# First-layer weight preparation and value pooling in a fused attention and two-layer feed-forward kernel: later value loads summed by GpSimd, weight slices in three steps

## The chip, the cores and the metric

The kernel runs on one core of a Trainium2 chip. The metric is the device time of one execution in microseconds (us). A core has TensorE (PE; its weight loads are listed as PEld), VectorE (DVE), ScalarE (ACT), GpSimd (POOL) and SyncE (SP), which issues the DMA transfers. Each engine works through its own instructions in the order in which the program emits them, and waits where an operand is not ready or a buffer is not free.

## The reference

Three stages follow each other. The attention pools keys and values over 8 neighbouring rows first:

```python
k_p = k.reshape(B, H, Sp, pool, D).mean(axis=3)      # B, H, S, D = 8, 8, 576, 64; pool = 8
v_p = v.reshape(B, H, Sp, pool, D).mean(axis=3)
scores = (1 / sqrt(D)) * q @ k_p.T                   # softmax over the 72 pooled keys
x = softmax(scores) @ v_p                            # then to 4608 tokens of width 512
```

Then come two feed-forward layers, 512 to 2048 to 512, with weights of their own:

```python
h = x @ w_in;   x = (h * clip(h + 3, 0, 6) / 6) @ w_out
h = x @ w_in2;  x = (P(h) / Q(h)) @ w_out2           # P cubic, Q = 1 + |b0||h| + |b1| h*h + 1e-6
```

## The kernel before, in words

**Tiling.** The 4608 tokens are handled in 9 blocks of 512. A feed-forward layer goes through the 16 slices m of the hidden width for each block: `hidden` (line 447) computes 128 hidden rows for 512 tokens with 12 matmuls, an activation follows on ACT and VectorE, and `out1` (line 473; `out2`, 553, in layer two) adds the slice to the four output banks with 12 matmuls, two steps later (LAG = 2). Matmuls are done on a high and a low part of each operand (names ending in h and l), three products each.

**The order of the work.** It is written out by hand. The program is a sequence of steps ("slots"), one per slice and block: steps 0 to 143 are layer one, 144 to 287 layer two, and steps -12 to -1 (PRE = 12) are a prologue in which the attention of the first block and the first weights are made ready. `at(kind, step, function, ...)` puts a piece of work on a list of a step, and `slot(s)` emits the lists in a fixed order. For s >= 0 it is: `dm` (loads), `hidden(s)`, `ex` (exponentials), the second half of the activation of s-1, `el` (pooling), `ld` (more loads), `pe` (transposes, scores, attention), `out1(s-2)`, `nz` (normalisation), `mid` (splits into high and low), `hi` (row maxima), the first half of the activation of s, then `c2`, `c1`, `c3` and `la`. For s < 0 it is dm, ld, el, pe, hi, ex, nz, c1, mid, c2, c3, la. What one engine does in a step follows this order, and nothing later passes it.

**Attention.** Query tiles (`load_q`) go through `scores` (line 333, PE), `highest` (348, VectorE), `exponentials` (355 to 361, ACT), `normalize` (369 VectorE, 370 and 376 GpSimd), `transposes` (385, PE), `split_p` (396 ACT, 397 and 401 VectorE), `attend` (414, PE) and `split_x` (425, 426). Values come in six chunks of 128 rows by 512 per batch. The first batch's chunks are loaded in step -12 (`load_v`, line 235, issued before the second weight slice) into halves of weight tiles that are not yet needed (`half`), and `pool_first_v` (273) sums eight rows with eight matmuls against the identity into a PSUM bank, two chunks in each of steps -11, -10 and -9. The profile counts each of these f32 matmuls as two. `split_v` (287, 288), `mask_v` (297, GpSimd) and `mask_rest` (308 to 313) then make `vh`, `vl` and `vr`, which `attend` reads. Later batches load each chunk into `vraw` (two buffers) one step ahead of `pool_v` (248, a VectorE reduction).

**Weights.** They come as 64-bit values and are decoded on the chip. A layer-one slice (32 of them: m = 0 to 15, w_in and w_out in turn, numbered i = 0 to 31) is loaded (`load_weights`, 148), decoded (`decode_a` 154 and `decode_r` 159, ACT), put together (`decode_b` 173 and 174, VectorE; `decode_c` 181, GpSimd) and split into high and low (`split_weights` 201 ACT, 203 GpSimd or VectorE). Slices 0 to 23 take three steps for this: c3 of step s-1, c1 of s, c2 of s+1, slice 23 without the last. Slices 24 to 31 go through `make_ready(i)`, all in c1 of one step: decode slice i, split slice i-1, put slice i together. Their loads are in `ld` of step s-1, and s = 2(i-11)/3 rounded down, so that four slices fall on three steps. Slices 24, 25, 28 and 29 are loaded into the two halves of the tile `y`, slices 26, 27, 30 and 31 into the two `raw64` buffers. All eight share the single buffer `t` (line 172) for the assembled value.

Of the kernel before, what the change touches and what calls it, by code (L numbers as in the profile page):

```python
# [19 lines left out]
F32 = mybir.dt.float32  # L20
F32R = mybir.dt.float32r
I32 = mybir.dt.int32
U32 = mybir.dt.uint32
I64 = mybir.dt.int64
AF = mybir.ActivationFunctionType
ALU = mybir.AluOpType
AX = mybir.AxisListType

B, H, S, D = 8, 8, 576, 64
POOLED = 8  # L30
SP = S // POOLED
NT, DM, DFF = B * S, H * D, 2048
P = 128
# [8 lines left out]
VCH = 6  # L42
# [26 lines left out]
def feed_forward_kernel(tc, q_t, k_t, v_r, vmask, w_in1, w_out1, w_in2, w_out2, a_rep, b_rep, out):  # L69
    nc = tc.nc  # L70

    const = tc.alloc_tile_pool(name="const", bufs=1)
    wpool = tc.alloc_tile_pool(name="weights", bufs=1)
# [4 lines left out]
    att = tc.alloc_tile_pool(name="att", bufs=1, side="right")  # L78
    dram = tc.alloc_tile_pool(name="spill", bufs=1, space=bass.MemoryType.DRAM)
    ps_y = tc.alloc_tile_pool(name="ps_y", bufs=1, space=bass.MemoryType.PSUM)  # L80
# [7 lines left out]
    ident = const.tile([P, P], F32, name="ident")  # L88
    vr = const.tile([P, 2, 2, 2, D], F32R, name="vr")
    kbd = const.tile([P, NPAIR, 2, SP], F32, name="kbd")  # L90
    mask = const.tile([P, 6], F32, name="mask")
# [32 lines left out]
    LATE = MF // 2  # L124
# [4 lines left out]
    def place(m, o):  # L129
        return wpool.tile([P, 2, DM], F32R, tag=f"w{m}{o}", name="w")  # L130

    def early(c):
        return c[0] == 0 and c[1] < AT_WORK
# [16 lines left out]
    def decode_a(*c):  # L150
        hi = raw[c].bitcast(I32).rearrange("p (n t) -> p n t", t=2)[:, :, 1].bitcast(F32)

        dec[c] = ps_h.tile([P, DM], F32, tag="h", name="d") if c[0] == 0 and 2 * c[1] + c[2] < PRE - 1 else hi
        nc.scalar.activation(out=dec[c], in_=hi, func=AF.Copy, scale=2.0 ** -112)

    def decode_r(*c):
        lo = raw[c].bitcast(I32).rearrange("p (n t) -> p n t", t=2)[:, :, 0]
        rnd[c] = lo
        nc.scalar.activation(out=lo, in_=lo.bitcast(U32), func=AF.Copy, scale=2.0 ** -29)
# [3 lines left out]
    def decode_b(*c):  # L163
        d = dec.pop(c).bitcast(I32)
        if early(c):
            i = 2 * c[1] + c[2]
            if i % 2 == 0:
                m, o = RAWS[NRAW + i // 2 % 2]
                turns[0] = wpool.tile([P, 2, DM], I32, tag=f"w{m}{o}", name="t")
            t = turns[0][:, i % 2, :]  # L170
        else:
            t = att.tile([P, DM], I32, tag="t", name="t")
        nc.vector.tensor_scalar(out=t, in0=d, scalar1=3, scalar2=None, op0=ALU.logical_shift_left)
        nc.vector.scalar_tensor_tensor(
            out=t, in0=d, scalar=-2 ** 31, in1=t, op0=ALU.bitwise_and, op1=ALU.bitwise_or
        )
        whole[c] = t

    def decode_c(*c):
        t = whole[c]  # L180
        nc.gpsimd.tensor_tensor(out=t, in0=t, in1=rnd.pop(c), op=ALU.add)  # L181
        whole[c] = t.bitcast(F32)
# [14 lines left out]
    def split_weights(*c):  # L197
        t = whole.pop(c)
        raw.pop(c)
        w = place(*c[1:])  # L200
        nc.scalar.activation(out=w[:, 0, :], in_=t, func=AF.Copy)
        eng = nc.gpsimd if c[2] or 2 * c[1] + c[2] >= PRE - 1 else nc.vector
        eng.tensor_tensor(out=w[:, 1, :], in0=t, in1=w[:, 0, :].bitcast(F32), op=ALU.subtract)
        for i, part in enumerate("hl"):
            wts[part][c] = w[:, i, :]


    q_sb, k_raw, v_raw, vh, vl = {}, {}, {}, {}, {}
# [16 lines left out]
    def half(name):  # L225
        if halves[1] % 2 == 0:
            i = halves[1] // 2
            halves[0] = wpool.tile([P, 2, DM], F32, tag=f"w{LATE + i // 2}{i % 2}", name=name)
        halves[1] += 1
        return halves[0][:, (halves[1] - 1) % 2, :]  # L230

    def load_v(b, c):
        t = half("v_raw") if b == 0 else att.tile([P, DM], F32, tag="vraw", bufs=2, name="v_raw")
        v_raw[b, c] = t.rearrange("p (r d) -> p r d", d=D)
        nc.sync.dma_start(out=t, in_=v_r[b, c])

# [5 lines left out]
    vsum = {}  # L242
# [23 lines left out]
            dst = kbd[rows, :, j, SM:SP] if p == NPAIR else kbd[rows, p, j, 0:SM]  # L266
            nc.vector.tensor_reduce(out=dst, in_=k[rows], axis=AX.X, op=ALU.add)

    def pool_first_v(c):
        if c == 0:  # L270
            vsum[0] = ps_y.tile([P, 512], F32, tag="y0", name="ps_vs")
        for r in range(POOLED):
            nc.tensor.matmul(
                vsum[0][:, c * D:(c + 1) * D], lhsT=ident, rhs=v_raw[0, c][:, r, :],
                start=r == 0, stop=r == POOLED - 1,
            )

    vparts = {}

    def split_v(b):  # L280
        src = vsum.pop(b)
        vs = src
        if b == 0:
            src = src[:, 0:VCH * D].rearrange("p (c d) -> p c d", d=D)
            vs = att.tile([P, VCH, D], F32, tag="vsum", name="vsum")
        vsh = att.tile([P, VCH, D], F32R, tag="vsh", name="vsh")
        nc.scalar.activation(out=vsh, in_=src, func=AF.Copy)
        nc.vector.tensor_tensor(
            out=vs[:, 0:4, :], in0=src[:, 0:4, :], in1=vsh[:, 0:4, :].bitcast(F32), op=ALU.subtract
        )  # L290
        vparts[b] = vsh.bitcast(F32), vs, src

    def mask_v(b, f, part):
        src, dst, nm = vparts[b][part], (vh, vl)[part], ("vh", "vl")[part]
# [9 lines left out]

    def mask_rest(b):

        hi, vs, src = (x[:, 4:6, :] for x in vparts[b])
        nc.vector.tensor_scalar(out=hi, in0=hi, scalar1=mask[:, 3:4], scalar2=None, op0=ALU.mult)
        nc.vector.scalar_tensor_tensor(
            out=vs, in0=src, scalar=mask[:, 2:3], in1=hi, op0=ALU.mult, op1=ALU.add  # L310
        )
        for i in range(2):
            nc.vector.tensor_scalar(
                out=vr[:, :, i, 1, :], in0=vs, scalar1=mask[:, 4 + i:5 + i], scalar2=None, op0=ALU.mult
            )
# [252 lines left out]
    pe, ex, el, nz, mid, hi, la, dm, ld, c1, c2, c3 = ({} for _ in range(12))  # L568

    def at(kind, slot, f, *a):  # L570
        kind.setdefault(slot, []).append(lambda: f(*a))
# [3 lines left out]
    chunks = [(m, o) for m in range(MF) for o in range(2)]  # L575

    def prepare_first(s0, units):

        at(dm, s0, load_q, *units[0])
        for p in (0, 1, NPAIR):  # L580
            at(dm, s0, load_first_k, p)
        at(dm, s0, load_weights, 0, *chunks[0])
        for u in units[1:3]:
            at(dm, s0, load_q, *u)
        for p in (2, 3):
            at(dm, s0, load_first_k, p)
        for c in range(VCH):
            at(dm, s0, load_v, 0, c)
            at(pe, s0 + 1 + c // 2, pool_first_v, c)
        at(dm, s0, load_weights, 0, *chunks[1])  # L590
        for p in (0, NPAIR, 1):
            at(el, s0, pool_first_k, p)
        for p in (2, 3):
            at(la, s0 + p - 2, pool_first_k, p)
        at(la, s0 + 3, split_v, 0)
        for i in range(4):
            at(la, s0 + 4 + i // 2, mask_v, 0, i // 2, i % 2)
        at(la, s0 + 4, mask_rest, 0)

    def prepare(b, k0, k1, a0, a1):  # L600

# [16 lines left out]
    for j in range(NB):  # L618
        s0 = MF * (j - 1)
# [6 lines left out]
        for us in groups:  # L626
            b, g, f, _ = us[0]
            for u in us + [None]:
                s = s0 + round(14 * k / (steps - 1)) if j else k + 2 - PRE
# [26 lines left out]
            prepare(j, k0, k1, a0, a1)  # L656


    def make_ready(i):
        if i < len(chunks):  # L660
            decode_a(0, *chunks[i])
            decode_r(0, *chunks[i])
        here = i < len(chunks) and early((0, *chunks[i]))
        if i > 0 and not here:
            split_weights(0, *chunks[i - 1])
        if i < len(chunks):
            decode_b(0, *chunks[i])
            decode_c(0, *chunks[i])
        if i > 0 and here:
            split_weights(0, *chunks[i - 1])  # L670

    for i in range(len(chunks) + 1):
        s = i + 1 - PRE if i < PRE - 1 else 2 * (i + 1 - PRE) // 3
        c = (0, *chunks[i]) if i < len(chunks) else None
        if c and i > 1:
            if i < 24:
                at(dm, max(s - 3, -PRE), load_weights, *c)
            else:
                at(ld, s - 1, load_weights, *c)
        if i < 24:  # L680

            at(c3, s - 1, decode_a, *c)
            at(c3, s - 1, decode_r, *c)
            at(c1, s, decode_b, *c)
            at(c1, s, decode_c, *c)
            if i < 23:
                at(c2, s + 1, split_weights, *c)
        else:
            at(c1, s, make_ready, i)


    SWITCH = T1 - MF
# [13 lines left out]
    for i, (m, o) in enumerate(chunks):  # L706
        s = 24 + 3 * i
        at(dm, s - 2, load_weights, 1, m, o)
        at(el, s, decode_a, 1, m, o)
        at(la, s + 1, decode_r, 1, m, o)  # L710
        at(la, s + 1, decode_b, 1, m, o)
        at(la, s + 2, decode_c, 1, m, o)
        at(la, s + 3, spill_weights, 1, m, o)
        at(dm, SWITCH + m + 1 + LAG * o, reload_weights, 1, m, o)
    for j in range(NB2):
        s = T1 + j * MF
# [127 lines left out]
```

## Time and profile before

| | us |
|---|---|
| median of 3 runs | 1764.97 |
| lowest and highest | 1764.26, 1765.46 |
| profiled execution | 1760.91 |
| its span, first to last instruction | 1759.2 |

The mean granted TensorE clock over the span is 0.989 of full speed. A row of a timeline reads: start in us, duration in us, engine, line, operation, output <- inputs, partitions x elements, how many; in brackets the idle time of the engine just before and what ended it. A row of the waits reads: who waited <- for whom: total us, how often, longest. A row of the chain of waits reads: start, duration, what. A row of the groups or of a windows view is explained where it stands.

### The profile page before, as it was taken

To read this page: it belongs to the slowest core of one execution; us is meant where nothing else is said; L and a number is where in the kernel's file an instruction comes from. 1 tells how busy PE (TensorE), PEld (TensorE's weight loads), DVE (VectorE), ACT (ScalarE), POOL (GpSimd) and SP (SyncE) were. 2 spreads that over 40 slices of the span, in tenths; PEclk is the share of its full clock that TensorE was granted. 3 is DMA by queue.
4 is the path that set the end of the run, shared out by engine and by line. 5 is a ranking of instruction groups with operands and counts; after the bars stand their busy time and mean duration, and the time that the engine had idled before them with its cause. 6 is when DMAs were issued, how large, how long until landed. Compare 5 with 4: busy or idle time off the path is not lost.

```text
span 1759.2 us, 22444 instructions
## 1 busy us (share of the span) xinstructions
PE 1712.7 (97%) x7824; PEld 1417.2 (81%) x7824; DVE 1065.9 (61%) x1743; ACT 986.5 (56%) x2226; POOL 750.7 (43%) x762
## 2 busy tenths in 40 slices
PE   6688999999999999999999999999999999999999
PEld 5477888888888888888888888888888888888887
DVE  5885546556474664644322666666666666666665
ACT  5776444555455555544322666666666666666665
POOL 4575021212112121211001666666666666767665
PEclk8799999999999999999999999999999999999999
DMA  6532313233241423312055201010101010101000
GB/s 208 176 128 75 94 51 131 77 112 108 86 142 58 140 88 105 118 65 70 13 181 207 91 7 42 7 43 7 42 7 42 7 42 7 44 6 43 1 25 24
DMA packets 68336, 128.33 MB, mean 73 GB/s; under 512 B 11392, under 2 KB 27776, under 8 KB 68224
## 3 DMA queue, kind: packets, MB, share of 16 engines
q1 hardware_dynamic: 68224, 126.91, 21.6%
q8 instruction: 62, 1.02, 0.2%
q14 instruction: 50, 0.41, 0.1%
HBM read 91.23 MB, written 35.65 MB: 72 GB/s over the span
## 4 chain that ended last, share of the span: by engine, by line
PE 90%; DVE 0%; ACT 0%; POOL 0%; issue 0%; DVEq 0%
PE ps_h L447 42%; PE ps_o L553 22%; PE ps_y L473 21%; PE ps_s L333 2%; PE ps_v L414 2%; PE ps_t L385 1%; ACT s L358 0%; POOL gl L539 0%; POOL t L181 0%; DVE t L515 0%; DVE g L530 0%; DVE r L526 0%; DVE qd L523 0%; DVE t L514 0%; ACT y L479 0%
## 5 line engine op out<-in xcount | busy, mean ns | idle before, releaser
L473 PE MATMUL ps_y<-gh,w 128*128 128x512 f32 x1152 | 388.6, 398 | 0.0
L447 PE MATMUL ps_h<-xh,w 128*128 128x512 f32 x1152 | 380.2, 391 | 5.2 <-DVE gl L462 5.2
L447 PE MATMUL ps_h<-x2h,w 128*128 128x512 f32 x1152 | 377.8, 389 | 0.8 <-DVE t L515 0.8
L553 PE MATMUL ps_o<-w,gh 128*128 128x512 f32 x1152 | 354.7, 389 | 0.0
L447 PEld LDWEIGHTS ps_h<-xh,w 128*128 128x128 f32 x1152 | 217.2, 189 | 51.1 <-DVE gl L462 5.8
L473 PEld LDWEIGHTS ps_y<-gh,w 128*128 128x128 f32 x1152 | 217.0, 188 | 46.3 <-issue 1.6
L447 PEld LDWEIGHTS ps_h<-x2h,w 128*128 128x128 f32 x1152 | 216.3, 188 | 46.1 <-DVE t L515 1.2
L553 PEld LDWEIGHTS ps_o<-w,gh 128*128 128x128 f32 x1152 | 216.3, 188 | 45.0
L370 POOL TENSOR_TENSOR s<-s,rc 128x128 f32<-128x128 f32 (+1 forms) x80 | 32.0, 400 | 501.8 <-DVE rc L369 439.4
L523 DVE SCALAR_TENSOR_TENSOR qd<-qd,r 128x512 f32<-128x512 f32 x144 | 99.0, 688 | 220.0 <-ACT r L522 204.4
L473 PE MATMUL ps_y<-gl,w 128*128 128x512 f32 x576 | 225.1, 391 | 0.0
L447 PE MATMUL ps_h<-xl,w 128*128 128x512 f32 x576 | 225.0, 391 | 0.1
L447 PE MATMUL ps_h<-x2l,w 128*128 128x512 f32 x576 | 224.1, 389 | 0.0
L553 PE MATMUL ps_o<-w,gl 128*128 128x512 f32 x576 | 224.1, 389 | 0.0
L510 POOL TENSOR_SCALAR qd<-ah,coef 128x512 f32<-128x512 f32 x144 | 111.3, 773 | 258.2 <-ACT ah L508 258.1
L462 DVE TENSOR_TENSOR gl<-ps_h,gh 128x512 fp32r<-128x512 f32 x144 | 99.4, 690 | 167.3 <-ACT gh L461 166.6
L539 POOL TENSOR_TENSOR gl<-g,gh 128x512 fp32r<-128x512 f32 x144 | 186.6, 1296 | 19.0 <-ACT gh L538 18.9
L513 POOL TENSOR_TENSOR qd<-qd,ah 128x512 f32<-128x512 f32 x144 | 187.1, 1299 | 12.1
L508 ACT ACTIVATE ah<-ps_h 128x512 f32<-128x512 f32 x144 | 86.1, 598 | 152.4 <-PE ps_h L447 152.4
L521 ACT ACTIVATE r<-qd,cst 128x512 f32<-128x512 f32 x144 | 99.6, 692 | 105.2 <-POOL qd L513 105.2
L461 ACT ACTIVATE gh<-ps_h 128x512 fp32r<-128x512 f32 x144 | 84.9, 590 | 113.4 <-PE ps_y L473 97.6
L455 DVE SCALAR_TENSOR_TENSOR ps_h<-r,ps_h 128x512 f32<-128x512 f32 x144 | 100.0, 694 | 75.1 <-ACT r L454 72.5
(87 smaller groups left out, 2646.2 us busy)
## 6 DMA issues: line engine op xcount, KB each, us to landing
raw<-w_in SPq DMA_DIRECT2D x32, 512.0 KB, 3.7
raw<-w_out SPq DMA_DIRECT2D x32, 512.0 KB, 3.7
w<-raw SPq DMA_DIRECT2D x32, 512.0 KB, 2.8
w<-w SPq DMA_DIRECT2D x32, 512.0 KB, 4.1
v_raw<-v_r SPq DMA_DIRECT2D x47, 256.0 KB, 4.0
y<-y SPq DMA_DIRECT2D x36, 256.0 KB, 2.9
x2r<-y SPq DMA_DIRECT2D x36, 256.0 KB, 2.9
out<-o SPq DMA_DIRECT2D x36, 256.0 KB, 2.2
```

The costliest lines, as they stand in the source:

```text
L447: nc.tensor.matmul(ps, lhsT=w, rhs=x, start=o == 0, stop=o == len(ops) - 1)
L455: nc.vector.scalar_tensor_tensor(out=ps, in0=r, scalar=1.0, in1=ps, op0=ALU.min, op1=ALU.mult)
L461: nc.scalar.activation(out=gh[it], in_=ps, func=AF.Copy)
L462: nc.vector.tensor_tensor(out=gl[it], in0=ps, in1=gh[it].bitcast(F32), op=ALU.subtract)
L473: nc.tensor.matmul(yp[j][c], lhsT=w, rhs=x, start=m == 0 and o == 0, stop=m == MF - 1 and o == 2)
L508: nc.scalar.activation(out=ah, in_=ps, func=AF.Abs)
L510: nc.gpsimd.tensor_scalar(out=qd, in0=ah, scalar1=absb[1], scalar2=absb[0], op0=ALU.mult, op1=ALU.add)
L513: nc.gpsimd.tensor_tensor(out=qd, in0=qd, in1=ah, op=ALU.mult)
L521: nc.scalar.activation(out=r0, in_=qd, func=AF.Ln, scale=2.0 ** -LN_SHIFT, bias=cst[:, 1:2])
L523: nc.vector.scalar_tensor_tensor(out=qd, in0=qd, scalar=1.0 + 1e-6, in1=r0, op0=ALU.add, op1=ALU.mult)
L539: nc.gpsimd.tensor_tensor(out=gl[it], in0=g, in1=gh[it].bitcast(F32), op=ALU.subtract)
L553: nc.tensor.matmul(yp[j][c], lhsT=w, rhs=x, start=m == 0 and o == 0, stop=m == MF - 1 and o == 2)
```

## The change

First value batch: `load_first_v(c)` loads two chunks into one whole weight tile (w10,1, then w11,0 and w11,1), and SP issues these loads behind the second weight slice, in steps -12, -11 and -10. `sum_first_v(c)` sums the eight rows of two chunks on GpSimd by three halvings (additions of 512, 256 and 128 elements per partition), at the end (`la`) of steps -11, -10 and -9. The pooling matmuls and their PSUM bank are gone. `split_v`, `mask_v` and `mask_rest` of this batch come one step later and read SBUF.

Late weight slices: `make_ready` is gone. Slices 23 to 31 follow the rule of the others: decode in c3 of step s-1, put together in c1 of s, split in c2 of s+1. The loads of slices 24 to 31 stay in `ld` of step s-1. `t` has two buffers, and `vraw` of the later batches has one instead of two.

```diff
-            t = att.tile([P, DM], I32, tag="t", name="t")
+            t = att.tile([P, DM], I32, tag="t", bufs=2, name="t")
...
+    def load_first_v(c):
+        i = c // 2 + 1
+        v_raw[0, c] = wpool.tile([P, 2, DM], F32, tag=f"w{LATE + 2 + i // 2}{i % 2}", name="v_raw")
+        for i in range(2):
+            nc.sync.dma_start(out=v_raw[0, c][:, i, :], in_=v_r[0, c + i])
...
-        t = half("v_raw") if b == 0 else att.tile([P, DM], F32, tag="vraw", bufs=2, name="v_raw")
+        t = att.tile([P, DM], F32, tag="vraw", name="v_raw")
...
-    def pool_first_v(c):
+    def sum_first_v(c):
         if c == 0:
-            vsum[0] = ps_y.tile([P, 512], F32, tag="y0", name="ps_vs")
-        for r in range(POOLED):
-            nc.tensor.matmul(
-                vsum[0][:, c * D:(c + 1) * D], lhsT=ident, rhs=v_raw[0, c][:, r, :],
-                start=r == 0, stop=r == POOLED - 1,
-            )
+            vsum[0] = att.tile([P, VCH, D], F32, tag="vsum", name="vsum")
+        t = v_raw.pop((0, c)).rearrange("p c (r d) -> p c r d", d=D)
+        n = POOLED // 2
+        while n:
+            dst = t[:, :, 0:n] if n > 1 else vsum[0][:, c:c + 2, :].unsqueeze(2)
+            nc.gpsimd.tensor_tensor(out=dst, in0=t[:, :, 0:n], in1=t[:, :, n:2 * n], op=ALU.add)
+            n //= 2
...
-        for c in range(VCH):
-            at(dm, s0, load_v, 0, c)
-            at(pe, s0 + 1 + c // 2, pool_first_v, c)
         at(dm, s0, load_weights, 0, *chunks[1])
+        for c in range(0, VCH, 2):
+            at(dm, s0 + c // 2, load_first_v, c)
+            at(la, s0 + 1 + c // 2, sum_first_v, c)
...
-        at(la, s0 + 3, split_v, 0)
+        at(la, s0 + 4, split_v, 0)
         for i in range(4):
-            at(la, s0 + 4 + i // 2, mask_v, 0, i // 2, i % 2)
-        at(la, s0 + 4, mask_rest, 0)
+            at(la, s0 + 5 + i // 2, mask_v, 0, i // 2, i % 2)
+        at(la, s0 + 5, mask_rest, 0)
...
-        if i < 24:
+        if True:
             at(c3, s - 1, decode_a, *c)
             at(c3, s - 1, decode_r, *c)
             at(c1, s, decode_b, *c)
             at(c1, s, decode_c, *c)
-            if i < 23:
-                at(c2, s + 1, split_weights, *c)
-        else:
-            at(c1, s, make_ready, i)
+            at(c2, s + 1, split_weights, *c)
```

More of the change, by code (lines that the diff above doesn't have):

```diff
@@ L267, in pool_first_k @@
             nc.vector.tensor_reduce(out=dst, in_=k[rows], axis=AX.X, op=ALU.add)
-    def pool_first_v(c):
+    def sum_first_v(c):
         if c == 0:
-            vsum[0] = ps_y.tile([P, 512], F32, tag="y0", name="ps_vs")
-        for r in range(POOLED):
-            nc.tensor.matmul(
-                vsum[0][:, c * D:(c + 1) * D], lhsT=ident, rhs=v_raw[0, c][:, r, :],
-                start=r == 0, stop=r == POOLED - 1,
-            )
+            vsum[0] = att.tile([P, VCH, D], F32, tag="vsum", name="vsum")
[5 more added lines that the diff above has]
+            n //= 2
     vparts = {}
     def split_v(b):
[L281 to L285, printed above, removed]
+        vs = vsum.pop(b)
         vsh = att.tile([P, VCH, D], F32R, tag="vsh", name="vsh")
-        nc.scalar.activation(out=vsh, in_=src, func=AF.Copy)
+        nc.scalar.activation(out=vsh, in_=vs, func=AF.Copy)
         nc.vector.tensor_tensor(
-            out=vs[:, 0:4, :], in0=src[:, 0:4, :], in1=vsh[:, 0:4, :].bitcast(F32), op=ALU.subtract
+            out=vs[:, 0:4, :], in0=vs[:, 0:4, :], in1=vsh[:, 0:4, :].bitcast(F32), op=ALU.subtract
         )
-        vparts[b] = vsh.bitcast(F32), vs, src
+        vparts[b] = vsh.bitcast(F32), vs
     def mask_v(b, f, part):
@@ L305, in mask_rest @@
     def mask_rest(b):
-        hi, vs, src = (x[:, 4:6, :] for x in vparts[b])
+        hi, vs = (x[:, 4:6, :] for x in vparts[b])
         nc.vector.tensor_scalar(out=hi, in0=hi, scalar1=mask[:, 3:4], scalar2=None, op0=ALU.mult)
         nc.vector.scalar_tensor_tensor(
-            out=vs, in0=src, scalar=mask[:, 2:3], in1=hi, op0=ALU.mult, op1=ALU.add
+            out=vs, in0=vs, scalar=mask[:, 2:3], in1=hi, op0=ALU.mult, op1=ALU.add
         )
@@ L656, in feed_forward_kernel @@
             prepare(j, k0, k1, a0, a1)
[L659 to L672, printed above, removed]
+    for i in range(len(chunks)):
         s = i + 1 - PRE if i < PRE - 1 else 2 * (i + 1 - PRE) // 3
-        c = (0, *chunks[i]) if i < len(chunks) else None
-        if c and i > 1:
+        c = (0, *chunks[i])
+        if i > 1:
             if i < 24:
```

## The prediction

> **What bounds the kernel now.** I read the page first, then the waits of TensorE (PE), once over the whole span and once from 180 us on.
>
> ```profile
> span 1759.2 us, 22444 instructions
> PE 1712.7 (97%) x7824; PEld 1417.2 (81%) x7824; DVE 1065.9 (61%) x1743; ACT 986.5 (56%) x2226; POOL 750.7 (43%) x762
> ```
> ```profile
> PE ps_t L385 <- POOL s L376: 9.3, 2, 6.2
> ...
> PE ps_s L333 <- ACT s L358: 6.4, 4, 2.6
> ```
> ```profile
> PE ps_h L447 <- DVE t L515: 0.8, 1, 0.8
> ```
>
> PE is busy 97% of the span. Its longest waits are for normalised scores in the prologue (first row of the second view); the 6.4 us for ACT are looked at below. The last row is everything PE waits for after 180 us. So every microsecond won or lost ahead of 180 us comes out at the end one for one, and a delay on another engine after that costs nothing until it reaches PE. The change can only pay in two places: the prologue (before the first hidden step, at about 65 us) and steps 0 to 14 of the first layer.
>
> Next I read PE's timeline for the idle time inside the steps, and ScalarE's (ACT's) at the same moments.
>
> ```profile
> 131.94 0.48 PE L414 MATMUL ps_v<-pth,vh 128*128 128x448 f32 x1 [1.15 <-ACT s L358]
> 147.71 0.70 PE L333 MATMUL ps_s<-kbd,q_sb 128*64 128x144 f32 x4 [2.56 <-ACT s L358]
> 163.29 1.33 PE L333 MATMUL ps_s<-kbd,q_sb 128*128 128x144 f32 x4 [2.58 <-ACT s L358]
> ```
> ```profile
> 129.81 0.63 ACT L201 ACTIVATE w<-t 128x512 fp32r<-128x512 f32 x1 [1.86 <-POOL t L181]
> 145.58 0.63 ACT L201 ACTIVATE w<-t 128x512 fp32r<-128x512 f32 x1 [2.90 <-POOL t L181]
> 161.16 0.63 ACT L201 ACTIVATE w<-t 128x512 fp32r<-128x512 f32 x1 [2.91 <-POOL t L181]
> ```
>
> Each of the three PE waits follows an ACT wait by a microsecond or two. `make_ready` puts a slice's split (L201) into the step in which GpSimd (POOL) adds that slice together. ACT stands still until POOL is done, the exponentials (L358) queued behind the split come late, and PE waits for the bank that they read. The chain of waits shows what the last of the three adds:
>
> ```profile
> 164.62 3.79 PE ps_y L473 x12
> ...
> 178.22 2.72 PE ps_y L473 x12
> ...
> 183.99 0.49 PE ps_s L333 x4
> 184.48 2.74 PE ps_y L473 x12
> ```
>
> After the wait of 2.58 us the score matmuls take 1.33 us instead of 0.49 and the twelve output matmuls 3.79 instead of 2.74: PE ran at a lower clock for a while. A step's period is 184.48 - 178.22 = 6.26 us.
>
> **The last eight slices in three steps.** With decode (ACT) in step s-1, bit work and add (VectorE, POOL) in s and split in s+1, no split follows its own add directly. The three waits, 1.15 + 2.56 + 2.58 = 6.29 us, lose their cause, and so do the slow matmuls, 0.84 + 1.05 = 1.89 us: 8.18 us in all. The second t buffer belongs to this. With one, VectorE's bit work waited for the previous slice's split:
>
> ```profile
> 147.58 0.43 DVE L173 TENSOR_SCALAR t<-raw 128x512 int32<-128x512 int32 x1 [3.45 <-POOL w L203]
> ```
>
> With two it waits for the split of the slice before that one, which lies in an earlier step or earlier in the same one.
>
> What is late next: loads keep their step s-1, but the decode moves into that same step. Slices 24 to 27 find fresh buffers, and SP runs ahead. Slice 28 takes over the tile of 24 and 25, whose last reader is 25's add:
>
> ```profile
> 138.51 1.30 POOL L181 TENSOR_TENSOR t<-t,raw 128x512 int32<-128x512 int32 x1 [1.32 <-issue]
> ```
> ```profile
> 139.84 0.33 SPq L148 DMA_DIRECT2D raw<-w_in  x1
> ```
> ```profile
> raw<-w_in SPq DMA_DIRECT2D x32, 512.0 KB, 3.7
> ```
>
> The load leaves at the end of the add and lands 3.7 us later. Carrying the durations of these rows through steps 9 and 10, I put the add's end 2.6 us into step 10, the landing at 6.3 us and ACT's arrival at that decode at 4.6 us: a new ACT wait of about 1.7 us (an estimate). Queued behind it are step 11's exponentials, whose bank PE wants about 3 us into step 11. That is nearly covered, and I charge 0.6 us, for it and for step 11, where ACT has two splits and two decodes. Bounds: nothing, and 2.56 us, the worst wait of the same shape today. Net for this part: 8.2 - 0.6 = **7.6 us won**.
>
> **The first values on POOL instead of PE.**
>
> ```profile
> 13.24 3.65 PE L273 MATMUL ps_vs<-k_raw,ident 128*128 128x64 f32 x16 [1.09 <-DMA k_raw<-v_r]
> ...
> 20.09 0.85 PE L385 MATMUL ps_t<-ident,s 128*128 128x128 f32 x3
> 20.73 1.17 PE L333 MATMUL ps_s<-kbd,q_sb 128*128 128x144 f32 x4
> ...
> 26.00 0.50 PE L385 MATMUL ps_t<-ident,s 128*128 128x128 f32 x3
> 26.34 0.66 PE L333 MATMUL ps_s<-kbd,q_sb 128*128 128x144 f32 x4
> ...
> 39.91 0.79 PE L414 MATMUL ps_v<-ptl,vh 128*128 128x512 f32 x1 [2.07 <-DVE ptl L397]
> ```
> ```profile
> 17.56 0.62 ACT L154 ACTIVATE d<-raw 128x512 f32<-128x512 f32 x1 [4.09 <-DMA raw<-w_out]
> 26.54 0.49 ACT L396 ACTIVATE pth<-ps_t 128x384 fp32r<-128x384 f32 x1 [1.68 <-PE ps_t L385]
> 30.55 0.49 ACT L287 ACTIVATE vsh<-ps_vs 128x384 fp32r<-128x384 f32 x1 [1.88 <-PE ps_vs L273]
> ```
> ```profile
> 6.89 0.43 SPq L235 DMA_DIRECT2D k_raw<-v_r  x1
> ...
> 11.79 0.40 SPq L148 DMA_DIRECT2D raw<-w_out  x1
> ```
>
> Today the pooling matmuls stand ahead of the first transposes (13.24 to 20.09 us). ACT also waits 4.09 us for the second weight slice, which SP issues behind six value loads. In SP's new order that slice leaves where the first value load left, 4.9 us sooner, so its 4.09 us go. The two other ACT waits also end on PE's pooling, directly or through the transposes behind it. This is up to 4.09 + 1.68 + 1.88 = 7.65 us on ACT, but POOL now takes the work over, and POOL decides when the masked values are there:
>
> ```profile
> 15.25 1.29 POOL L181 TENSOR_TENSOR t<-t,raw 128x512 int32<-128x512 int32 x1 [0.15 <-DVE t L174]
> ...
> 30.20 1.27 POOL L203 TENSOR_TENSOR w<-t,w 128x512 fp32r<-128x512 f32 x1
> 33.24 0.40 POOL L370 TENSOR_TENSOR s<-s,rc 128x128 f32<-128x128 f32 x1 [1.77 <-DVE rc L369]
> 33.72 0.67 POOL L376 TENSOR_TENSOR s<-s,rc 128x288 f32<-128x288 f32 x1
> ...
> 42.09 0.62 POOL L297 TENSOR_TENSOR vh<-vsh,mask 128x256 fp32r<-128x256 f32 x1
> ...
> 51.58 1.74 POOL L181 TENSOR_TENSOR t<-t,raw 128x512 int32<-128x512 int32 x1
> ```
> ```profile
> L513 POOL TENSOR_TENSOR qd<-qd,ah 128x512 f32<-128x512 f32 x144 | 187.1, 1299 | 12.1
> ```
>
> No f32 add of this kind runs on POOL today; its nearest rows have the same sizes. A pair of chunks costs three adds of 512, 256 and 128 elements, 1.29 + 0.62 + 0.40, and two steps from one dependent POOL instruction to the next, 12.1 / 144 = 0.08 us each: 2.47 us. Three pairs cost 7.4 us. In POOL's new order, from the end of the first add (15.25 + 1.29 = 16.54 us) to the first masked value, stand the three sums (7.4), four normalisations of 0.40 + 0.67 (4.3), four decode adds of 1.29 (5.2), two splits of 1.27 (2.5) and the mask (0.62): 20.0 us, to 36.6 us. One wait for the reciprocal, as the 1.77 us above, is likely on the way: 38.3 us. Before, the attention matmuls began at about 37 us but stood still again until 39.91. Their second matmul would now come at about 38.9 us: 1.0 us sooner.
>
> From there to 65 us ACT goes on as before, so I take **1.0 us won**. If POOL never waits the gain is 2.7 us. If its sums run at the slowest rate shown, 1.74 / 1.29 = 1.35 times, 2.6 us come on top and it is a loss of 1.6 us. I take a value near the middle because the POOL rows around 15 to 45 us mostly have their short durations. That the split and mask of these values stand one step later is in this order; that they read SBUF instead of a PSUM bank moves tenths of a microsecond on ACT and VectorE.
>
> On the sums the Trainium skill speaks against the change: "GPSIMD Engine Reference", Engine selection, has elementwise work on VectorE, GpSimd being about twice as slow. By that rule the sums would belong on VectorE, and POOL's order above would be 7.4 us shorter. No row here has an f32 add of one size on both engines.
>
> **One buffer for later value chunks.**
>
> ```profile
> L248 DVE TENSOR_REDUCE vsum<-v_raw x42: 1039/1070/1130, 69.8 to 733.3; 128x64 f32<-128x512 f32 x42
> ...
> DMA to landing us min/median/max: 2.5/4.0/6.4
> ```
>
> Each load now waits on SP for VectorE's reduction of the chunk before, which stands earlier in the same step. Behind it on SP are the next step's query and weight loads. Load, landing and reduction take 0.43 + 4.0 + 1.07 = 5.5 us, under the period of 6.26 us. What covers it is VectorE's slack, and I cost it at nothing. If it were gone the price is the excess times 42 chunks (below).
>
> **Sum.** 7.6 + 1.0 = 8.6 us. On the profiled execution (1760.91 us, span 1759.2) this gives 1752.3 us with a span of 1750.6. The runs' median stands 4.1 us above the profiled execution, and I carry the difference over: 1764.97 - 8.6 = **1756.4 us**. About 0.2%, 3.5 us, is what can be told from no change here.
>
> **Rivals.** First, POOL is the new bound of the prologue at the slow rate: +1.6 instead of -1.0, so 1764.97 - 7.6 + 1.6 = 1759.0 us. For it: POOL gets 7.4 us more just where the normalisations must feed PE. Against it: most rows are at the short durations.
>
> Second, the clock. The pooling kept PE busy from 13 us to 30 us, and it goes.
>
> ```profile
> 30.00:40.00 10.00, 4.05 (x21) 3.02 (x20) 7.65 (x18) 9.29 (x38) 6.88 (x10) 0.68 0.40 132
> ```
>
> Transposes and scores took 0.85 + 1.17 us at 20 us and 0.50 + 0.66 us at 26 us, after a stretch of dense matmuls. Without the pooling three steps keep the longer durations: 3 x 0.86 = 2.6 us, if all of it is on the path, so 1759.0 us. Against it: the granted clock was 0.68 from 30 to 40 us anyway, and ACT, not PE, is nearly full there. The Trainium skill, "TensorE: Matmul & The Clock Gate", What's actually happening, says that the default state is the throttled one and that about 3.4 us of sustained activity lift it. By that rule the slow durations stay; the rows at 20 and 26 us agree.
>
> Third, the loads take back the late slices' gain. If ACT stands the full 3.7 us at slice 28 and again at 30, which takes over 26's buffer, two waits like the 2.56 us stay, 5.1 us of 8.2: 1764.97 - 3.1 - 1.0 = 1760.9 us, and without the prologue's gain about 1762. For it: load and decode share a step. Against it: 26's and 27's adds no longer queue behind single t buffers.
>
> Fourth, on the other side: one value buffer. It decides where a landing takes longer than 6.26 - 1.07 - 0.43 = 4.8 us; the longest was 6.4. If they ran at 5.4 us, 0.6 us x 42 = 25 us would come on PE once VectorE's slack is used up: 1756.4 + 25 = 1781 us. Against it: DMA is light after 180 us, and VectorE is busy only 61%.
>
> **How the numbers follow.** Forecast 0.62, slow POOL 0.14, clock 0.06, loads 0.12, value buffer 0.06. The range takes in the bounds of the parts (8.2 + 2.7 = 10.9 us won; with the other slow stretches of steps 0 to 8 moving too, some 2 us more) and the loads rival: 1752 to 1762. Over 0.2% faster means below 1761.4 us: the first three and a part of the fourth, 0.81. The rest of the loads rival and a tenth of the forecast's tail give 0.13 within 0.2%, the value buffer 0.06 slower.
>
> **What would show it.** Right: no PE wait for ACT s between 125 and 165 us, no ACT wait at L201 over 1 us there, and ACT's 4.09 us at 17.56 gone; POOL's sums at about 2.5 us a pair; first hidden step at about 63.7 us instead of 64.7. Wrong: PE waits of over 1 us in steps 8 to 14 that end on a weight load, a first hidden step later than 66 us, or PE waits after 180 us.

## The result and the profile after

| | before | after |
|---|---|---|
| median of 4 runs, us | 1764.62 | 1752.76 |
| lowest to highest | 1762.67 to 1765.46 | 1752.60 to 1754.96 |
| profiled execution | 1760.91 | 1752.68 |
| its span | 1759.2 | 1750.9 |

The ratio is 0.9936 (95% interval 0.9923 to 0.9949): about 11.3 us faster, 11.9 by the medians, where 8.6 had been forecast. The two spans differ by 8.3 us only. The profiled execution of before, 1760.91 us, lies below every other run of that kernel on record (the lowest is 1761.02); that of after lies at its median. Where the other 3 to 4 us are is the main question below. Three executions far off all others (1926.87 and 9315.47 us of before, 2157.55 us of a later kernel) are left out of every figure.

From the page of after:

```profile
span 1750.9 us, 22245 instructions
PE 1698.0 (97%) x7728; PEld 1403.5 (80%) x7728; DVE 1073.1 (61%) x1743; ACT 986.3 (56%) x2226; POOL 759.1 (43%) x771
```

PE has 96 instructions less, POOL 9 more. The waits of PE in after, over the whole span:

```profile
PE ps_t L389 <- POOL s L380: 14.6, 4, 4.8
...
PE ps_v L418 <- POOL vh L301: 5.1, 1, 5.1
...
PE ps_s L337 <- ACT s L362: 1.8, 2, 1.1
PE ps_h L451 <- DVE t L519: 0.8, 1, 0.8
```

The waits of the scores for ACT fell from 6.4 to 1.8 us. The last row is again all that there is after 180 us. In the prologue PE now waits for POOL instead of pooling. The waits left in steps 8 to 14, from PE's timeline:

```profile
119.42 0.50 PE L451 MATMUL ps_h<-xh,w 128*128 128x512 f32 x1 [2.13 <-DVE gl L466]
143.46 0.70 PE L337 MATMUL ps_s<-kbd,q_sb 128*64 128x144 f32 x4 [0.78 <-ACT s L362]
```

The 1.15, 2.56 and 2.58 us of before are gone. ACT's waits at the splits, 1.86, 2.90 and 2.91 us before, are at most 1.38 us:

```profile
125.12 0.63 ACT L201 ACTIVATE w<-t 128x512 fp32r<-128x512 f32 x1 [1.38 <-POOL t L181]
```

PE's 0.78 us is the new wait, and ACT, SP and POOL show its cause:

```profile
140.74 0.68 ACT L154 ACTIVATE raw<-raw 128x512 f32<-128x512 f32 x1 [2.74 <-DVE t L173]
```
```profile
137.03 0.33 SPq L148 DMA_DIRECT2D raw<-w_in  x1
```
```profile
135.70 1.30 POOL L181 TENSOR_TENSOR t<-t,raw 128x512 int32<-128x512 int32 x1 [0.63 <-DVE t L174]
```

POOL's add of slice 25 ends at 137.00, SP issues slice 28's load at 137.03, and its decode starts 3.7 us later, the time that such a load takes to land. The label names VectorE, whose bit work on slice 27 ends 0.02 us before that decode:

```profile
140.30 0.42 DVE L173 TENSOR_SCALAR t<-raw 128x512 int32<-128x512 int32 x1
```

Slice 28's decode does not read what that instruction writes. In six kernels below with the same order (late slices alone, matmuls put back, loads undone, the two with sums on VectorE, mask later) the same wait carries the load's label, and the decode starts 3.65 to 3.90 us after SP issues the load. In the kernel with the late slices alone ACT's row and the chain of waits pass through the load itself:

```profile
143.61 0.67 ACT L154 ACTIVATE raw<-raw 128x512 f32<-128x512 f32 x1 [2.87 <-DMA raw<-w_in]
```

```profile
138.45 1.31 POOL t L181
139.78 3.75 DMA raw<-w_in
143.57 0.04 issue
143.61 0.10 ACT raw L154
```

### The profile page after: what moved, and what is told of

It reads as the page before. It is cut to its first block, busy times and chain, and to the rows that moved or that the text cites. A ratio compares the mean times of both kernels' runs of the same rounds, so it can differ in the third digit from the quotient of the medians.

```text
span 1750.9 us, 22245 instructions
## 1 busy us (share of the span) xinstructions
PE 1698.0 (97%) x7728; PEld 1403.5 (80%) x7728; DVE 1073.1 (61%) x1743; ACT 986.3 (56%) x2226; POOL 759.1 (43%) x771
## 4 chain that ended last, share of the span: by engine, by line
PE 93%; DVE 4%; DMA 1%; ACT 1%; POOL 1%; issue 0%; SPq 0%; POOLq 0%; ACTq 0%; DVEq 0%
PE ps_h L451 43%; PE ps_o L557 22%; PE ps_y L477 22%; PE ps_s L337 2%; PE ps_v L418 2%; PE ps_t L389 1%; DVE t L174 1%; DMA raw<-w_in 1%; DVE t L173 1%; DVE vsum L254 0%; DVE ps_h L459 0%; DMA v_raw<-v_r 0%; DVE kbd L246 0%; DVE nm L352 0%; ACT s L362 0%
```

## Experiments

Starts of hidden steps, read from PE's timeline (us), and spans:

| kernel | step 0 | step 8 | step 15 | 8 to 15 | span |
|---|---|---|---|---|---|
| before | 64.71 | 120.49 | 175.34 | 54.85 | 1759.2 |
| before, second profile | 64.64 | 121.05 | 178.36 | 57.31 | 1762.5 |
| before, third profile | 68.34 | 124.23 | 179.12 | 54.89 | 1763.4 |
| late slices only | 64.49 | 120.61 | 169.72 | 49.11 | 1754.1 |
| first values only | 64.59 | 118.72 | 173.56 | 54.84 | 1758.2 |
| after | 65.01 | 119.42 | 166.83 | 47.41 | 1750.9 |
| all three additions | 61.94 | 114.18 | 160.94 | 46.76 | 1745.1 |

Differences from after, below, compare medians of separate rounds of runs. The median of before moved by 0.9 us between those rounds (1764.26 to 1765.14), so a difference of less than about 1 us settles nothing.

My theory was that the late slices carry the gain; the rival, that the first values give a good part of it.

**The late slices alone** (before, with the change's edits to the last eight slices, `t` and `vraw`).

```diff
-            t = att.tile([P, DM], I32, tag="t", name="t")
+            t = att.tile([P, DM], I32, tag="t", bufs=2, name="t")
...
-            at(c1, s, make_ready, i)
+            at(c2, s + 1, split_weights, *c)
```

> Only the late slices change: three steps for slices 23 to 31, two t buffers, one buffer for later value chunks; the first values stay on TensorE. Theory (the late slices carry the gain): the three TensorE waits for ACT s between 125 and 165 us (1.15, 2.56, 2.58 us) and the slow matmuls after the last are gone, 7 to 8 us faster than before, the first hidden step at about 64.7 us as before. Rival (a good part of the measured 11.9 us is the first values' doing): only 4 to 6 us faster than before.

Measured: ratio 0.9955 (0.9939 to 0.9971), about 7.9 us (5.1 to 10.8). The three waits are gone, with a new one of 0.91 us for slice 28's load; the first hidden step starts at 64.49 us. Its 49.11 us from step 8 to 15 contain a stretch at half clock from about 121 us on: step 8 to 9 takes 8.20 us, against 6.60 in the first profile of before. The new schedule and the second `t` buffer were not tried apart.

**The first values alone** (after, with `make_ready`, one `t` and two `vraw` as before).

```diff
-            t = att.tile([P, DM], I32, tag="t", bufs=2, name="t")
+            t = att.tile([P, DM], I32, tag="t", name="t")
...
+            at(c1, s, make_ready, i)
```

> Only the first values change: loads behind the second weight slice, sums on GpSimd, split and mask one step later; late slices in one step with one t buffer and two value buffers, as before. Theory: the prologue ends where it did (first hidden step within 0.7 us of 64.7 us), steps 0 to 8 give about 1 us, so 0 to 2 us faster than before, and the three waits of 1 to 2.6 us in steps 9 to 13 stay. Rival: 3 to 5 us faster than before.

Measured: 0.9978 (0.9967 to 0.9989), about 3.9 us (1.9 to 5.8). The three waits are there unchanged:

```profile
130.17 0.48 PE L418 MATMUL ps_v<-pth,vh 128*128 128x448 f32 x1 [1.15 <-ACT s L362]
145.94 0.70 PE L337 MATMUL ps_s<-kbd,q_sb 128*64 128x144 f32 x4 [2.56 <-ACT s L362]
161.52 0.97 PE L337 MATMUL ps_s<-kbd,q_sb 128*128 128x144 f32 x4 [2.58 <-ACT s L362]
```

The rival of this text holds: the parts add up, 7.9 + 3.9 = 11.8, and the first values give about four times what I had put down, nearly twice at the least. The late slices remain the larger part.

**One buffer for the later values alone** (before, with this line).

```diff
-... att.tile([P, DM], F32, tag="vraw", bufs=2, name="v_raw")
+... att.tile([P, DM], F32, tag="vraw", name="v_raw")
```

> The kernel before with one buffer for later value chunks instead of two, nothing else. Theory (load, landing and reduction of 5.5 us fit into a step of 6.26 us): within 1 us of before, no TensorE wait after 180 us beyond the 0.8 us there today. Rival (one buffer exposes the loads): slower by 5 to 25 us, with TensorE waits spread over 180 to 900 us.

Measured: 1.0002 (0.9993 to 1.0010), and 0.8 us of PE waiting after 180 us. The theory holds.

**The kernel before, profiled twice more** (no edit).

> The kernel before, unchanged, for more of its executions and a second profile. The first profiled execution took 1760.91 us against a median of 1764.6. Theory (its executions differ by some us in the first 180 us, where the TensorE clock changes): the second profile shows the same waits in steps 8 to 14, and its span differs from 1759.2 us by the place where TensorE stands or runs slowly before 180 us. Rival: the difference lies after 180 us.

> The kernel before, a third profile. Theory (its executions differ by the clock: the moment at which the rise comes during the pooling matmuls, and the number of slow windows of 3.4 us after the waits of steps 8 to 14): the span is explained by these two, with each slow window costing about 1.7 us and each microsecond by which the rise comes later about half a microsecond. Rival: the span differs for another reason at the same clock.

The profiled executions took 1764.21 and 1765.09 us, medians 1764.66 and 1765.38. The second profile is 3.3 us longer than the first, of which 3.0 us are there by step 15. A windows view of it (window, length, then PE, PEld, DVE, ACT, POOL busy, granted clock, DMA share, GB/s) shows the clock:

```profile
122.40:125.60 3.20, 3.20 (x10) 2.07 (x8) 1.27 (x2) 0.00 (x0) 3.20 (x4) 0.50 0.00 0
149.70:152.90 3.20, 3.20 (x9) 2.36 (x8) 2.94 (x7) 3.17 (x9) 2.47 (x4) 0.50 0.10 24
166.80:170.00 3.20, 3.20 (x10) 2.61 (x9) 3.12 (x7) 2.72 (x6) 1.57 (x2) 0.50 0.03 5
```

From step 8 on PE runs at half clock three times here, against once in the first profile. From step 8 to 15 this makes 57.31 - 54.85 = 2.5 us, about 1.2 us for each of the two further windows where the theory had 1.7. The third profile differs elsewhere: hidden step 0 starts 3.6 us later. PE's timeline there:

```profile
16.02 3.62 PE L273 MATMUL ps_vs<-v_raw,ident 128*128 128x64 f32 x16
...
21.03 6.93 PE L273 MATMUL ps_vs<-v_raw,ident 128*128 128x64 f32 x32
...
29.35 4.47 PE L273 MATMUL ps_vs<-v_raw,ident 128*128 128x64 f32 x32
...
64.79 0.77 PE L414 MATMUL ps_v<-pth,vh 128*128 128x512 f32 x1 [2.77 <-ACT sm L361]
```

And the same groups in the first profile:

```profile
21.69 4.48 PE L273 MATMUL ps_vs<-v_raw,ident 128*128 128x64 f32 x32
...
26.83 3.68 PE L273 MATMUL ps_vs<-v_raw,ident 128*128 128x64 f32 x32
...
61.48 0.77 PE L414 MATMUL ps_v<-pth,vh 128*128 128x512 f32 x1 [2.76 <-ACT sm L361]
```

The 32 matmuls took 6.93 us instead of 4.48, then 4.47 instead of 3.68: the clock rose some 8 us later. These differences add up to 3.2 of the 3.3 us by which the second attention starts later (64.79 - 61.48). That it is the clock is read from the durations. The granted clock of the windows view (1.00 and 0.50 below) does not show this first rise; but the transposes and scores at 20 us take 0.85 and 1.17 us, about as long as those at 34 us (0.90 and 1.17), where it reads 0.50:

```profile
20.00:22.00 2.00, 2.00 (x11) 2.00 (x11) 0.07 (x1) 1.55 (x6) 0.00 (x0) 1.00 0.47 186
34.00:36.00 2.00, 1.56 (x7) 1.51 (x7) 1.96 (x4) 1.97 (x10) 1.91 (x3) 0.50 0.30 121
```
```profile
34.44 0.90 PE L385 MATMUL ps_t<-ident,s 128*128 128x128 f32 x3 [3.10 <-POOL s L376]
35.14 1.17 PE L333 MATMUL ps_s<-kbd,q_sb 128*128 128x144 f32 x4
```

In five profiles with this prologue's matmuls and order (three of before, the late slices alone, the single value buffer) it rose early three times and late twice. The theory's two causes hold; its "half a microsecond per microsecond" fits (8 us later, 3.3 to 3.6 us longer).

**PE's matmuls put back, the sums left on GpSimd** (after, with the 96 identity matmuls on a constant at their old places, results unread).

```diff
+                nc.tensor.matmul(
+                    vsum["pe"][:, (c + i) * D:(c + i + 1) * D], lhsT=ident, rhs=ident[:, 0:D],
...
+            at(pe, s0 + 1 + c // 2, idle_matmuls, c)
```

> The changed kernel, with the 96 identity matmuls of before put back in TensorE's order at their old places, on a constant instead of the values, their results unread; the sums stay on GpSimd. Theory (what the first values win is that TensorE's dense f32 matmuls leave the prologue, which at the low clock take 3.6 us for 16 and push back transposes and scores): slower than the changed kernel by 2 to 4 us, 1755 to 1757 us, and with a wider spread between executions, since the moment at which the clock rises differs. Rival (the earlier weight slice and ScalarE's shorter waits win it): within 1 us of the changed kernel.

Measured: 1759.02 us (1757.43 to 1760.36), 6.3 us above after: the theory's direction, more than its size; the spread is hardly wider. The transposes come late:

```profile
11.98 6.93 PE L280 MATMUL ps_vs<-ident 128*128 128x64 f32 x32
18.70 0.85 PE L399 MATMUL ps_t<-ident,s 128*128 128x128 f32 x3
...
20.30 6.93 PE L280 MATMUL ps_vs<-ident 128*128 128x64 f32 x32
27.02 0.85 PE L399 MATMUL ps_t<-ident,s 128*128 128x128 f32 x3
...
28.62 4.01 PE L280 MATMUL ps_vs<-ident 128*128 128x64 f32 x32
...
66.40 0.76 PE L428 MATMUL ps_v<-pth,vh 128*128 128x512 f32 x1 [2.76 <-ACT sm L375]
```

The second attention starts at 66.40 us, in after at 61.46. Hidden step 0 starts 4.9 us later than in after (69.95 us), steps 0 to 8 take 55.80 us instead of 54.41, and steps 8 to 15 take the same (47.51 and 47.41): 4.9 + 1.4 = 6.3 us, the whole difference.

**The order of the loads undone** (after, all six value loads ahead of the second weight slice).

```diff
+        for c in range(0, VCH, 2):
+            at(dm, s0, load_first_v, c)
         at(dm, s0, load_weights, 0, *chunks[1])
         for c in range(0, VCH, 2):
-            at(dm, s0 + c // 2, load_first_v, c)
```

> The changed kernel, with all six value loads issued ahead of the second weight slice again. Theory (the earlier weight slice counts little, because GpSimd decides when the masked values are there): ScalarE waits about 4 us for the second slice again, GpSimd's second normalisation comes about 1.7 us later, and the time is 0 to 2 us above the changed kernel's. Rival (the load order is what the first values' part wins): 3 to 5 us above it.

Measured: 1755.16 us (1752.82 to 1756.11), 2.4 us above after: a little over the theory's range and under the rival's. Hidden step 0 starts at 66.81 us, 1.8 later, as the second normalisation's 1.7 us had it. The order of the loads is a part of the first values' gain, smaller than that of the matmuls. The two prices, 6.3 + 2.4 = 8.7 us, exceed the 3.9 us that the first values gave. The sums on GpSimd, which this kernel and the last one keep, take time of their own; how much of the 8.7 us they take back was not measured.

**The sums on VectorE, all or the third pair** (after, with a reduction of two chunks in place of the three adds, always or for c = 4).

```diff
+        nc.vector.tensor_reduce(
+            out=vsum[0][:, c:c + 2, :], in_=t.rearrange("p c r d -> p c d r"), axis=AX.X, op=ALU.add
+        )
```

> The changed kernel, with each of the three GpSimd sums replaced by one VectorE reduction of two chunks at the same places in the order. Theory (GpSimd's 7.7 us of sums hold up the third and fourth normalisation, 4.8 us of TensorE waiting, and the masked values): about 2.1 us each on VectorE, the masked values 1 to 2 us sooner, 0 to 2.5 us faster than the changed kernel. Rival (VectorE, the fuller engine there, becomes the bound): 1 to 3 us slower.

> The changed kernel, with only the third pair of chunks summed by one VectorE reduction; the first two pairs stay on GpSimd. VectorE stood idle for 2.9 us just there. Theory: GpSimd's fourth normalisation and ScalarE's copy of the sums come 2 to 3 us sooner, and with them the attention and the first hidden step: 1.5 to 3 us faster than the changed kernel. Rival (the prologue is bound elsewhere after that, by ScalarE's exponentials): under 0.7 us.

Measured: 1752.74 us (all) and 1752.13 us (third pair), against 1752.76. Step 0 starts at 62.83 and 62.17 us, 2.2 and 2.8 us sooner, as the theories said, but both times are within 1 us of after's, which the rival of the second text had for the third pair. A reduction of two chunks takes 1.9 us, against 2.6 us for the three adds on GpSimd:

```profile
24.53 1.93 DVE L281 TENSOR_REDUCE vsum<-v_raw 128x128 f32<-128x1024 f32 x1
```

Most of the prologue's gain is lost at step 8, not on ACT as that rival had it. There PE waits 2.44 us for VectorE in the third-pair kernel (2.13 in after) and then runs at half clock, which it does not in after:

```profile
116.78 0.53 PE L456 MATMUL ps_h<-xh,w 128*128 128x512 f32 x1 [2.44 <-DVE gl L471]
```
```profile
117.20:120.40 3.20, 3.20 (x9) 2.52 (x8) 2.16 (x4) 1.02 (x2) 3.12 (x4) 0.50 0.00 0
```

Its step 8 to 9 takes 8.20 us instead of 6.64: of the 2.6 us by which step 8 starts sooner, 1.1 are left at step 9. In the kernel with all sums on VectorE 1.6 us shrink to 0.1 in the same way.

**VectorE's mask of the second batch one step later** (after).

```diff
-        at(la, a1, mask_rest, b)
+        at(la, a1 + (b == 1), mask_rest, b)
```

> The changed kernel, with the second batch's mask_rest (four VectorE instructions, 2.65 us just ahead of the subtraction that frees hidden step 8's bank) one step later. Theory (what is late next in steps 0 to 8 is VectorE, and a wait of about 2 us costs its own length and, in some executions, a slow clock window of 3.4 us at half rate): TensorE's wait of 2.13 us at 119 us is gone and 1.5 to 3 us are won. Rival (the wait only moves to the next hidden step): under 0.7 us.

Measured: 1751.59 us (1750.88 to 1752.34), 1.2 us won, a little under the theory's range. The wait of 2.13 us is gone; steps 7 to 8 take 5.44 us instead of 7.73. In its profile step 8 starts 2.8 us sooner than in after, step 15 only 1.95 us sooner; of the 0.8 us lost in between, 0.6 fall on step 9 to 10, which takes 7.71 us instead of 7.10. Why it does was not separated.

**The decode of slices 28 to 31 in the step in which they are put together** (after).

```diff
-            at(c3, s - 1, decode_a, *c)
-            at(c3, s - 1, decode_r, *c)
+            late = i >= 28
+            at(c2 if late else c3, s if late else s - 1, decode_a, *c)
+            at(c2 if late else c3, s if late else s - 1, decode_r, *c)
```

> The changed kernel, with the decode of slices 28 to 31 one step later, in the step in which they are put together, ahead of it. Theory (ScalarE's 2.74 us before slice 28's decode is a wait for its load, which starts at the end of the add of slice 25): that wait and TensorE's 0.78 us at 143.5 us are gone, 0.5 to 1 us won. Rival (the profile's label, VectorE, is the cause, or VectorE now waits for the decode): no change, or up to 2 us slower.

Measured: a median of 1752.46 us (1751.20 to 1753.51), 0.3 below after, which is no difference that can be told from none. ACT's 2.74 us and PE's 0.78 us are gone, and steps 9 to 15 take 39.91 us instead of 40.77, the 0.5 to 1 us of the theory. A later decode would have outlived a VectorE wait as well, so this alone does not name the cause; the load's label in the six kernels above does. The profiled execution, the longest of the four, lost the gain again: a slow window at 119.4 us makes its step 8 to 9 last 7.95 us.

**All three** (third pair on VectorE, mask later, decode later).

> The changed kernel with the third pair of chunks summed on VectorE, mask_rest of the second batch one step later and the decode of slices 28 to 31 one step later. If the three gains add up: first hidden step at about 62.2 us, no TensorE wait over 1 us between 76 and 180 us, 1747 to 1749 us. If slow clock windows take part of it back: 1749.5 to 1752 us.

Measured: 1747.23 us (1746.94 to 1747.33), ratio to before 0.9900 (0.9884 to 0.9915): 5.5 us below after. Alone the three gave 0.6, 1.2 and 0.3 us, the largest just beyond what the rounds differ by. Together, PE's waits for the hidden steps' banks and for ACT's scores are:

```profile
PE ps_h L456 <- DVE gl L471: 1.9, 1, 1.9
PE ps_s L342 <- ACT s L367: 1.1, 1, 1.1
```

There is none between 85 and 180 us, and no slow window after 89 us. The time is that of three gains that add up in their stages.

## Why the prediction came out as it did

The direction was right, and the measured 1752.76 us lies in the range of 1752 to 1762, near its lower end and 3.6 us below the forecast. One of the two terms was mis-sized. That the spans differ by 8.3 us where 8.6 was forecast is in part luck: step 0 came 0.3 us later instead of 1.0 sooner, and steps 0 to 8 gave 1.4 us that the sum did not hold (from step 8 to 15 came 7.4).

**Late slices, 8.2 - 0.6 = 7.6 us: right.** Alone they gave 7.9 us. In the first profiles steps 8 to 15 went from 54.85 to 47.41 us, 7.4 less. The new wait for slice 28's load was there: on ACT 2.74 us where 1.7 had been estimated, on PE 0.78 us where 0.6 had been charged. One sign was missed: a wait at L201 of over 1 us is left, the 1.38 us at 125 us. The rival in which the loads take the gain back fell.

**First values, 1.0 us: wrong in size, 3.9 us measured.** The failed step is the comparison itself: I set POOL's new order against the one execution that I had, in which the clock rose at about 23 us, and carried its 4.1 us below the median over as a constant. POOL's order was nearly as worked out:

```profile
16.64 2.08 POOL L283 TENSOR_TENSOR v_raw<-v_raw 128x512 f32<-128x512 f32 x2
18.80 0.45 POOL L283 TENSOR_TENSOR vsum<-v_raw 128x128 f32<-128x128 f32 x1
...
30.31 1.00 POOL L283 TENSOR_TENSOR vsum<-v_raw 128x128 f32<-128x128 f32 x1
...
38.75 0.67 POOL L301 TENSOR_TENSOR vh<-vsh,mask 128x256 fp32r<-128x256 f32 x1
```

A pair takes 2.6 us (2.47 forecast), the last one 0.5 us more, and the masked values are there at 39.4 us instead of 38.3. So against that execution the prologue won nothing: the second attention started at 61.46 us, before at 61.48, and the first hidden step at 65.01 us, where 63.7 had been named as the sign of being right. Against one whose clock rises late it won 3.3 us. In steps 0 to 8 another 1.4 to 2.3 us came (54.1 to 54.4 us instead of 55.8 to 56.4), which I had not counted. With the matmuls put back these steps take 55.80 us again, so by this one profile the gain there goes with the matmuls; how they act so late was not separated.

That the split and mask read SBUF had been put at tenths of a microsecond. On VectorE (L288, 308, 309 and 313, now L292, 312, 313 and 317) they took 3.8 us instead of 1.9. Why is open: in later batches, which read SBUF in both kernels, two of these rows have medians of 0.42 and 0.35 us, where the first batch now took 0.80 and 1.17. It did not reach PE, which waited for POOL's mask until 39.47 us.

**The clock rival had the wrong sign.** I priced the loss of PE's warm-up at 2.6 us. The transposes and scores did keep their longer durations, in after:

```profile
25.78 0.90 PE L389 MATMUL ps_t<-ident,s 128*128 128x128 f32 x3 [3.50 <-POOL s L380]
26.47 1.17 PE L337 MATMUL ps_s<-kbd,q_sb 128*128 128x144 f32 x4
```

But the matmuls that warmed PE were themselves on the path, 32 of them in 6.93 us for 3.68 later: putting them back cost 6.3 us. The Trainium skill, "TensorE: Matmul & The Clock Gate", What's actually happening, has the clock rise after about 3.4 us of sustained activity. Here PE was dense from 13 us on, and the rise came some 10 us later, or 18, so here it took longer than the Trainium skill states.

**Slow POOL and the single value buffer** did not come: the sums ran at their short durations but for one, and the buffer alone measured 1.0002. Nor did moving the sums to VectorE show in the time: there they took 1.9 instead of 2.6 us a pair and brought the first hidden step 2.2 us forward, but the time stayed (1752.74). A row of one size on both engines was there to be read: the split's subtraction (L203) took 1.26 us at its shortest on POOL and 0.68 on VectorE.

## What to carry to other kernels

Where TensorE bounds the kernel, a split that directly follows its own add on another engine costs twice, by its wait and by what queues behind it; giving each its own step, with a second buffer, removed both here. Before a kernel's profile is used as a base line, see where that execution lies among the others. Dense small matmuls put into a prologue to use an idle TensorE may run at their long durations (here 6.93 us instead of 3.68) and hold up what is queued behind them. Judge an edit by the stage it touches as well as by the time: one that loses its gain to a slow window can still be right together with others.

## What the runs showed of the hardware

A TensorE wait of 1.6 to 2.6 us was followed by 3.4 us at half clock in some executions and not in others. With the same instructions, the wait before step 8 was not followed by one in the first profile of before, and was in the second (its window at 122.40 us is shown above):

```profile
120.49 0.50 PE L447 MATMUL ps_h<-xh,w 128*128 128x512 f32 x1 [2.46 <-DVE gl L462]
```
```profile
121.05 0.50 PE L447 MATMUL ps_h<-xh,w 128*128 128x512 f32 x1 [2.44 <-DVE gl L462]
```

The shortest such wait, in after, and its window (5.6 us at a mean of 0.70 is 3.4 us at 0.50, the rest at full clock):

```profile
87.56 0.30 PE L418 MATMUL ps_v<-pth,vh 128*128 128x64 f32 x1 [1.64 <-ACT s L362]
```
```profile
86.40:92.00 5.60, 4.44 (x14) 3.69 (x15) 5.57 (x10) 4.78 (x17) 3.81 (x5) 0.70 0.65 206
```

One such window cost 1.3 to 1.6 us (step 8 to 9: 7.95 and 8.20 us with it, 6.64 without). The clock's first rise, as the durations show it under the same dense matmuls, came at about 23 us in one execution and 31 us in another.
